# Explicit scheduler priorities, and three ordering rules at the start, in an attention + MLP kernel on one Trainium2 core

## The chip, the cores and the metric

The kernel runs on one core of one Trainium2 chip. Times are device microseconds (us). A verdict compares the fast-state executions of two kernels that ran on the same chip in the same rounds; executions of one kernel here spread over about 1% (355.8 to 360.2 us for the kernel before), so differences under about 1 us are not settled by these runs. Engine names in the profile: PE is TensorE's matmuls, PEld its weight loads, DVE VectorE, ACT ScalarE, POOL GpSimd, SP the engine that issues most DMAs.

## The reference, cut to what matters

```python
# 4 batches, 8 heads, 768 positions, head dimension 64
ub    = sum(max(q*k_min, q*k_max))          # bound of each key chunk of 32, causal
sel   = the 6 chunks with the largest bound, per query
attn  = softmax(mask(scale * q @ k.T, sel and causal)) ; x = attn @ v
x     = x reordered to (4*768 tokens, 512)
h     = x @ w_in                             # 512 -> 2048
g     = where(h > 0, h, exp(min(h, 0)) - 1)  # called ELU below
out   = g @ w_out                            # 2048 -> 512, float32
```

## The kernel before

The work is cut into 8 blocks: 4 batches times 2 halves of 384 query positions. Each block goes through a *front* (K and Q are transposed on TensorE, the chunk bounds `ub` are computed, VectorE selects the chunks), an *attention* (scores `sps`, exponential `pt` on ScalarE, product `o3` with V) and an *MLP* (16 groups `fc` of 4 matmuls into `h_ps`, an ELU over three engines, then 48 matmuls into `o_ps`). The code is traced once; a scheduler orders each engine's instructions at build time, by priority (so far, the order of the code) and by its own model of when data will be ready. How the chip keeps to that order is read from the traces below: in the kernel before, GpSimd stands 22.1 us at one instruction of its order, and a later one that is ready from 35.3 us on starts only at 47.67 us.

```python
    ldpool = pool("ldpool", 4)     # loads of K, Q, V: 4 tiles each
    psM = pool("psM", 4, space=bass.MemoryType.PSUM)     # h_ps and o_ps share 4 banks
    ...
    def cast_v(t, hf):             # V to bfloat16, on GpSimd
        return nc.gpsimd.tensor_scalar(out=vexts[t % NSET][...], in0=ldv.pop((t, hf)), ...)
    ...
    def mlp(b, hf):
        for fc in range(NFC):      # 16
            for kk in range(NKK):  # 4
                nc.tensor.matmul(hw, lhsT=w_in_sb[...], rhs=xT[NPAIR * b + kk, hf], ...)   # L310
            nc.scalar.activation(out=e_sb, in_=hw, func=AF.Exp)                            # L313
            nc.gpsimd.tensor_scalar(out=e_sb, in0=e_sb, scalar1=-1.0, ...)                 # L314
            nc.vector.scalar_tensor_tensor(out=gT[:, fc, :], in0=hw, in1=e_sb, ...)        # L316
        for tt in range(3):
            for fc in range(NFC):
                nc.tensor.matmul(o_ps, lhsT=gT[...], rhs=w_out_sb[:, fc, :], ...)          # L321
            nc.scalar.activation(out=o_sb, in_=o_ps, func=AF.Copy)                         # L324
            nc.sync.dma_start(out=out[r0:r0 + P, :], in_=o_sb)
    ...
    front(0); casts = vpart(0)                       # vpart: the four cast_v of a block
    # load w_in, w_out behind casts[1] and casts[3] on GpSimd's queue
    for i in range(8):
        # attend(block i)
        # load V of block i+1;  front(i+1), which first loads K, Q of block i+2
        # mlp(block i-1)
        # vpart(i+1)
```

The softmax here doesn't subtract the row's maximum and nothing guards it: scores larger than these inputs give would overflow.

Of the kernel before, what the change touches and what calls it, by code (L numbers as in the profile page):

```python
# [25 lines left out]
P = 128  # L26
# [7 lines left out]

NPAIR = H // 2
PE_T = (0, 7)
NSET = 8
Q0 = TOPK * CHUNK
QLO = (Q0, HS)
# [4 lines left out]
def kernel(  # L44
# [31 lines left out]
    nc.scalar.activation(out=warm, in_=warm, func=AF.Exp)  # L76


    def load_one(x, t, hf, name, eng=None):
        b, r = divmod(t, NPAIR)  # L80
        xp = ldpool.tile([P, 3, 2, D], F32, name=name)
        for h in range(2):
            (eng or nc.sync).dma_start(out=xp[:, :, h, :],
                              in_=x[b, 2 * r + h, HS * hf:HS * (hf + 1)].rearrange("(n p) d -> p n d", p=P))
        return xp

    ldk, ldq, ldv = {}, {}, {}

    def load_qk(t, hf):
        ldk[t, hf] = load_one(k, t, hf, "k_pair")  # L90
        ldq[t, hf] = load_one(q, t, hf, "q_pair", nc.scalar if (t < 2 and hf == 0) else nc.sync)

    def load_v(t, hf):
        ldv[t, hf] = load_one(v, t, hf, "v_pair")

    for t in range(NPAIR):
        load_qk(t, 0)
# [52 lines left out]
    wo = moe_w_out.rearrange("(k p) f -> p k f", p=P)  # L150

    def load_w_in(i):
        nc.gpsimd.dma_start(out=w_in_sb[:, :, 512 * i:512 * (i + 1)], in_=wi[:, :, 512 * i:512 * (i + 1)])

    def load_w_out(i):
        nc.gpsimd.dma_start(out=w_out_sb[:, 4 * i:4 * i + 4, :], in_=wo[:, 4 * i:4 * i + 4, :])
# [80 lines left out]
             1: [[(0, 384, 384, 0)], [(1, 384, 384, 0)], [(2, 384, 384, 0)],  # L237
                 [(3, 384, 384, 0), (5, 640, 128, 384)], [(4, 512, 256, 0)]]}

    def attend(t, hf, via_pe):  # L240
        s = t % NSET
        xt = xtpool.tile([P, HS], BF16, name="xt")
        xT[t, hf] = xt
        seg = {}
        for segs in steps[hf]:
            wtot = max(pc + w for (_k, _c, w, pc) in segs)
            pt = ptpool.tile([P, 2, 512], BF16, name="pt")
            both = wtot <= 256
            for hd in range(2):
                if not (both and hd == 1):  # L250
                    sps = psS.tile([P, 512], F32, name="sps")
                o = 256 * hd if both else 0
                for (kb, c0, w, pc) in segs:
                    nc.tensor.matmul(sps[:, o + pc:o + pc + w], lhsT=lhs[s][hd][0:96, P * kb:P * (kb + 1)],  # L254
                                     rhs=rhs[s][hd][0:96, c0:c0 + w], start=True, stop=True)
                if not both:
                    nc.scalar.activation(out=pt[:, hd, 0:wtot], in_=sps[:, 0:wtot],  # L257
                                         func=AF.Exp, scale=SCALE)
            if both:
                nc.scalar.activation(out=pt[:, :, 0:256],  # L260
                                     in_=sps[:, :].rearrange("p (h w) -> p h w", h=2),
                                     func=AF.Exp, scale=SCALE)
            dg = [pc for (kb, c0, w, pc) in segs if c0 == P * kb]
            if len(dg) == 2:
                view = pt[:, :, :].rearrange("p h (x w) -> p h x w", w=P)[:, :, ::3, :]
                nc.vector.tensor_tensor(  # L266
                    out=view, in0=view,
                    in1=tri01[:, :].rearrange("p (a b w) -> p a b w", a=1, b=1)
                    .to_broadcast([P, 2, 2, P]), op=AOT.mult)
            elif dg:  # L270
                view = pt[:, :, dg[0]:dg[0] + P]
                nc.vector.tensor_tensor(  # L272
                    out=view, in0=view,
                    in1=tri01[:, :].rearrange("p (a w) -> p a w", a=1).to_broadcast([P, 2, P]),
                    op=AOT.mult)
            for (kb, c0, w, pc) in segs:
                seg[kb] = (pt, pc - c0)
        o3 = psO.tile([P, 2, 3, D + 1], F32, name="o3")
        for hd in range(2):
            for qi in range(3):  # L280
                qt = 3 * hf + qi
                for kb in range(qt + 1):
                    pt, off = seg[kb]
                    nc.tensor.matmul(o3[:, hd, qi, :],  # L284
                                     lhsT=pt[:, hd, P * qt + off:P * qt + off + P],
                                     rhs=vexts[s][:, kb, hd, :], start=(kb == 0), stop=(kb == qt))
        rcp = opool.tile([P, 2, 3, 1], F32, name="rcp")
        nc.vector.reciprocal(out=rcp, in_=o3[:, :, :, D:D + 1])
        on = opool.tile([P, 3, 2, D], BF16, name="on")
        nc.vector.tensor_tensor(out=on[:, :, :, :].rearrange("p q h d -> p h q d"),  # L290
                                in0=o3[:, :, :, 0:D],
                                in1=rcp[:, :, :, :].to_broadcast([P, 2, 3, D]), op=AOT.mult)
        if via_pe:
            pool0 = (psM, "psm") if (t < NPAIR and hf == 0) else (psT, "ps")
            pxt = pool0[0].tile([P, HS], BF16, name="pxt", tag=pool0[1])
            for qi in range(3):
                nc.tensor.transpose(pxt[:, P * qi:P * (qi + 1)], on[:, qi, :, :], ident_b)
            nc.vector.tensor_copy(out=xt, in_=pxt)
            return
        nc.sync.dma_start_transpose(out=xt[:, :].rearrange("p (n t) -> p n t", n=3),  # L300
                                    in_=on[:, :, :, :].rearrange("p q h d -> p (q h d)"))


    def mlp(b, hf):
        gT = gtpool.tile([P, NFC, HS], BF16, name="gT")
        for fc in range(NFC):
            h_ps = psM.tile([P, 512], F32, name="h_ps", tag="psm")
            hw = h_ps[:, 0:HS]
            for kk in range(NKK):
                nc.tensor.matmul(hw, lhsT=w_in_sb[:, kk, P * fc:P * (fc + 1)],  # L310
                                 rhs=xT[NPAIR * b + kk, hf], start=(kk == 0), stop=(kk == NKK - 1))
            e_sb = mlppool.tile([P, HS], F32, name="e_sb")
            nc.scalar.activation(out=e_sb, in_=hw, func=AF.Exp)  # L313
            nc.gpsimd.tensor_scalar(out=e_sb, in0=e_sb, scalar1=-1.0, scalar2=1.0,  # L314
                                    op0=AOT.add, op1=AOT.mult)
            nc.vector.scalar_tensor_tensor(out=gT[:, fc, :], in0=hw, scalar=0.0, in1=e_sb,  # L316
                                           op0=AOT.max, op1=AOT.min)
        for tt in range(3):
            o_ps = psM.tile([P, DMODEL], F32, name="o_ps", tag="psm")
            for fc in range(NFC):  # L320
                nc.tensor.matmul(o_ps, lhsT=gT[:, fc, P * tt:P * (tt + 1)], rhs=w_out_sb[:, fc, :],  # L321
                                 start=(fc == 0), stop=(fc == NFC - 1))
            o_sb = mlppool.tile([P, DMODEL], F32, name="o_sb", bufs=2)
            nc.scalar.activation(out=o_sb, in_=o_ps, func=AF.Copy)  # L324
            r0 = b * S + hf * HS + P * tt
            nc.sync.dma_start(out=out[r0:r0 + P, :], in_=o_sb)


    blocks = [(b, hf) for b in range(B) for hf in range(2)]

    def pairs_of(b):
        return range(NPAIR * b, NPAIR * (b + 1))

    def front(i):
        b, hf = blocks[i]
        if i + 1 < len(blocks):
            b1, hf1 = blocks[i + 1]
            for t in pairs_of(b1):
                load_qk(t, hf1)
        for t in pairs_of(b):  # L340
            prep(t, hf)
            if i == 0 and t % 2 == 0:
                if t == 0:
                    nc.vector.tensor_copy(out=econst[64:96], in_=eone[64:96].to_broadcast([32, NCH, CHUNK]))
                init_set(t)
                init_set(t + 1)
            if t % 2 == 1:
                select(t // 2, hf)

    def vpart(i):  # L350
        b, hf = blocks[i]
        return [cast_v(t, hf) for t in pairs_of(b)]

    for t in pairs_of(0):
        load_v(t, 0)
    front(0)
    casts = vpart(0)
    with tc.issue_after(casts[1].ins):
        load_w_in(0)
        load_w_in(1)  # L360
    with tc.issue_after(casts[3].ins):
        load_w_in(2)
        load_w_in(3)
        for i in range(4):
            load_w_out(i)
    for i in range(len(blocks)):
        for t in pairs_of(blocks[i][0]):
            attend(t, blocks[i][1], i in PE_T)
        if i == 0:
            for s in range(4, NSET):  # L370
                init_set(s)
        if i + 1 < len(blocks):
            b1, hf1 = blocks[i + 1]
            for t in pairs_of(b1):
                load_v(t, hf1)
            front(i + 1)
        if i >= 1:
            mlp(*blocks[i - 1])
        if i + 1 < len(blocks):
            vpart(i + 1)  # L380
    mlp(*blocks[-1])


# [28 lines left out]
```

## Time and profile before

355.88 us (median of 3, 355.84 to 360.23).

| | PE | DVE | ACT | POOL | mean clock of TensorE |
|---|---|---|---|---|---|
| busy, us of 354.8 | 305.1 (86%) | 220.8 (62%) | 228.6 (64%) | 98.0 (28%) | 0.947 |

Where the time lies in the span is read first. These are lines of the page's second part for the kernel before: the span in 40 slices of 8.9 us, each digit the busy share of a slice in tenths, and below the granted clock and the DMA share (9 is 90% or more).

```profile
PE   4577149799987899998998799998998899999995
POOL 8850065212103310244103310213104311331440
PEclk9855858899999999999999999999999999999999
DMA  7999976644654333251424223222321001000102
```

The fifth digit of PE is 1: a hole from about 36 to 44 us, with GpSimd at 0 in the same slice and the one before it, the DMA share at 9 (1.22 by the windows view of 38 to 42 us), and the clock at half in three slices between 18 and 53 us (the digits 5). The timeline of TensorE in the kernel before shows the hole itself (start, length, line, what it is, count, and in brackets the idle time before it with what ended it).

```profile
36.27 0.55 PE L192 MATMUL psQ<-ident_f,q_pair 128*128 128x128 f32 x3
36.65 0.33 PE L310 MATMUL h_ps<-xt,w_in_sb 128*128 128x384 bf16 x1
48.83 1.44 PE L310 MATMUL h_ps<-xt,w_in_sb 128*128 128x384 bf16 x4 [11.85 <-DVE gT L316]
```

TensorE stops after 16 matmuls of the first MLP, which is 4 groups, as many as `psM` has banks. It waits for `gT`, which frees a bank. `gT` needs GpSimd's `e_sb`, so GpSimd's timeline is next.

```profile
22.47 0.15 POOL L125 MEMSET vext_171<- 128x12 bf16 x1
44.73 0.51 POOL L159 TENSOR_SCALAR vext_129<-v_pair 128x384 bf16<-128x384 f32 x1 [22.11 <-DMA v_pair<-in_v_dram]
...
47.67 0.51 POOL L314 TENSOR_SCALAR e_sb<-e_sb 128x384 f32<-128x384 f32 x1
```

GpSimd stands at the cast of block 1's V from 22.6 to 44.7 us because that V has not landed. The MLP's `e_sb`, whose input ScalarE had finished at 35.3 us, is behind four such casts in GpSimd's order. GpSimd kept to that order in this trace: the `e_sb`, ready at 35.3 us, started at 47.67 us.

Later in the span the losses are smaller. The windows view of the kernel before, over two whole blocks (from the end of one MLP to the end of the next but one), gives busy time and count of each engine, clock, DMA share and GB/s.

```profile
218.90:297.10 78.20, 72.48 (x577) 39.18 (x575) 52.24 (x166) 55.90 (x127) 16.28 (x32) 1.00 0.20 51
```

And one line of TensorE's timeline in it: 42 `o_ps` matmuls in one run, while ScalarE has nothing but `o_sb` to do.

```profile
252.20 9.24 PE L321 MATMUL o_ps<-w_out_sb,gT 128*128 128x512 bf16 x42
```

### The profile page before, as it was taken

What the parts mean: (1) busy time and instruction counts of PE and PEld (TensorE: products, weight loads), DVE (VectorE), ACT (ScalarE), POOL (GpSimd) and SP (SyncE); (2) the same over time, 40 slices, a digit from 0 to 9 for tenths busy, and PEclk for the clock granted to TensorE, in tenths of its full rate; (3) what the DMA queues carried; (4) which work ended last, traced back from release to release, by engine and by line L of the source; (5) the groups of instructions that cost most, each with busy time, mean ns of one, the idle gap of its engine ahead of it and who ended that gap; (6) DMA issues with size and microseconds to landing.
All of it is one profiled execution on the core that took longest, in us unless ns stands there. A gap on an engine that the chain in (4) does not pass through costs nothing.

```text
span 354.8 us, 6831 instructions
## 1 busy us (share of the span) xinstructions
PE 305.1 (86%) x2328; PEld 165.1 (47%) x2328; DVE 220.8 (62%) x690; ACT 228.6 (64%) x506; POOL 98.0 (28%) x219
## 2 busy tenths in 40 slices
PE   4577149799987899998998799998998899999995
PEld 2344024355554444555455345555454445554552
DVE  6877027875659786568748874559747963562450
ACT  5652306889588755998559754998458736982541
POOL 8850065212103310244103310213104311331440
PEclk9855858899999999999999999999999999999999
DMA  7999976644654333251424223222321001000102
GB/s 177 178 202 196 211 167 137 144 100 102 173 141 91 68 71 119 59 133 35 102 84 86 58 68 108 56 47 59 87 72 22 2 30 61 1 3 31 59 5 84
DMA packets 94498, 32.16 MB, mean 91 GB/s; under 512 B 87296, under 2 KB 91392, under 8 KB 94464
## 3 DMA queue, kind: packets, MB, share of 16 engines
q1 hardware_dynamic: 88640, 27.15, 31.9%
q0 software_dynamic: 4224, 4.19, 7.1%
q10 hardware_dynamic: 1600, 0.39, 0.5%
q8 instruction: 18, 0.29, 0.3%
q14 instruction: 16, 0.13, 0.1%
HBM read 27.26 MB, written 6.29 MB: 95 GB/s over the span
## 4 chain that ended last, share of the span: by engine, by line
PE 33%; ACT 16%; DVE 8%; issue 2%; POOL 1%; ACTq 0%; POOLq 0%
PE o_ps L321 18%; PE h_ps L310 7%; ACT pt L257 6%; ACT e_sb L313 3%; PE sps L254 3%; DVE gT L316 2%; PE ub L214 2%; ACT pt L260 2%; PE psK L173 1%; POOL e_sb L314 1%; PE psQ L192 1%; ACT QTf L193 1%; DVE kmm L175 1%; ACT o_sb L324 1%; DVE on L290 1%
## 5 line engine op out<-in xcount | busy, mean ns | idle before, releaser
L310 PE MATMUL h_ps<-xt,w_in_sb 128*128 128x384 bf16 x512 | 113.5, 336 | 17.2 <-DVE gT L316 17.0
L314 POOL TENSOR_SCALAR e_sb<-e_sb 128x384 f32<-128x384 f32 x128 | 65.1, 516 | 190.9 <-ACT e_sb L313 158.3
L316 DVE SCALAR_TENSOR_TENSOR gT<-h_ps,e_sb 128x384 bf16<-128x384 f32 x128 | 69.1, 550 | 52.2 <-POOL e_sb L314 50.4
L321 PE MATMUL o_ps<-w_out_sb,gT 128*128 128x512 bf16 x384 | 90.1, 379 | 0.0
L257 ACT ACTIVATE pt<-sps 128x384 bf16<-128x384 f32 (+1 forms) x160 | 80.1, 547 | 11.4 <-PE sps L254 10.5
L313 ACT ACTIVATE e_sb<-h_ps 128x384 f32<-128x384 f32 x128 | 61.0, 498 | 36.7 <-PE h_ps L310 36.0
L310 PEld LDWEIGHTS <-w_in_sb 128*128 128x128 bf16 x512 | 49.1, 100 | 50.5 <-issue 29.0
L321 PEld LDWEIGHTS <-gT 128*128 128x128 bf16 x384 | 36.8, 98 | 42.3 <-issue 3.5
L324 ACT ACTIVATE o_sb<-o_ps 128x512 f32<-128x512 f32 x24 | 14.3, 597 | 53.8 <-PE o_ps L321 50.0
L284 PEld LDWEIGHTS <-pt 128*128 128x128 bf16 x672 | 29.2, 100 | 17.2 <-DVE pt L266 5.7
L173 PE MATMUL psK<-ident_f,k_pair 128*128 128x128 f32 x96 | 19.2, 306 | 8.7 <-DMA k_pair<-in_k_dram 6.1
L175 DVE TENSOR_REDUCE kmm<-psK 128x12 f32<-128x384 f32 x32 | 17.6, 551 | 6.9 <-PE psK L173 6.3
L266 DVE TENSOR_TENSOR pt<-pt,tri_196 128x512 bf16<-128x512 bf16 x32 | 13.5, 421 | 12.8 <-ACT pt L257 12.6
L192 PE MATMUL psQ<-ident_f,q_pair 128*128 128x128 f32 x96 | 18.2, 295 | 3.7 <-ACT lhs_167 L178 0.8
L260 ACT ACTIVATE pt<-sps 128x512 bf16<-128x512 f32 x32 | 19.4, 606 | 1.2 <-PE sps L254 0.9
L173 PEld LDWEIGHTS psK<-ident_f,k_pair 128*128 128x128 f32 x96 | 11.6, 152 | 16.4 <-issue 5.1
L193 ACT ACTIVATE QTf<-psQ 128x192 f32<-128x192 f32 (+1 forms) x32 | 13.4, 418 | 8.3 <-PE psQ L192 7.9
L192 PEld LDWEIGHTS psQ<-ident_f,q_pair 128*128 128x128 f32 x96 | 10.7, 145 | 16.0 <-ACT lhs_143 L178 2.8
L196 DVE TENSOR_SCALAR Qrl<-QTf 128x192 f32<-128x192 f32 (+1 forms) x32 | 10.3, 323 | 11.7 <-ACT QTf L193 11.1
L176 DVE TENSOR_REDUCE kmm<-psK 128x12 f32<-128x384 f32 x32 | 17.5, 548 | 0.0
L217 DVE STREAM_TRANSPOSE ubT<-ub 128x192 f32<-128x192 f32 (+1 forms) x16 | 7.6, 478 | 10.1 <-PE ub L214 10.1
L272 DVE TENSOR_TENSOR pt<-pt,tri_196 128x256 bf16<-128x256 bf16 x32 | 9.8, 306 | 4.6 <-ACT pt L260 3.8
(348 smaller groups left out, 403.1 us busy)
## 6 DMA issues: line engine op xcount, KB each, us to landing
k_pair<-in_k_dram SPq DMA_DIRECT2D x64, 96.0 KB, 2.5
v_pair<-in_v_dram SPq DMA_DIRECT2D x64, 96.0 KB, 2.4
out_dram<-o_sb SPq DMA_DIRECT2D x24, 256.0 KB, 2.0
q_pair<-in_q_dram SPq DMA_DIRECT2D x60, 96.0 KB, 2.5
w_in_sb<-in_moe_w_in_dram POOLq DMA_DIRECT2D x4, 512.0 KB, 9.9
w_out_sb<-in_moe_w_out_dram POOLq DMA_DIRECT2D x4, 512.0 KB, 20.2
q_pair<-in_q_dram ACTq DMA_DIRECT2D x4, 96.0 KB, 2.9
xt<-on SPq DMA_TRANSPOSE x24, 2.3
```

Of the source, the lines that this page charges most:

```text
L173: nc.tensor.transpose(ps[:, P * n:P * (n + 1)], k_pair[:, n], ident_f)
L175: nc.vector.tensor_reduce(out=kmm[:, 0, :], in_=pv, axis=AX.X, op=AOT.min)
L192: nc.tensor.transpose(ps[:, P * n:P * (n + 1)], q_pair[:, n], ident_f)
L257: nc.scalar.activation(out=pt[:, hd, 0:wtot], in_=sps[:, 0:wtot], func=AF.Exp, scale=SCALE)
L260: nc.scalar.activation(out=pt[:, :, 0:256], in_=sps[:, :].rearrange("p (h w) -> p h w", h=2), func=AF.Exp, scale=SCALE)
L284: nc.tensor.matmul(o3[:, hd, qi, :], lhsT=pt[:, hd, P * qt + off:P * qt + off + P], rhs=vexts[s][:, kb, hd, :], start=(kb == 0), stop=(kb ...
L310: nc.tensor.matmul(hw, lhsT=w_in_sb[:, kk, P * fc:P * (fc + 1)], rhs=xT[NPAIR * b + kk, hf], start=(kk == 0), stop=(kk == NKK - 1))
L313: nc.scalar.activation(out=e_sb, in_=hw, func=AF.Exp)
L314: nc.gpsimd.tensor_scalar(out=e_sb, in0=e_sb, scalar1=-1.0, scalar2=1.0, op0=AOT.add, op1=AOT.mult)
L316: nc.vector.scalar_tensor_tensor(out=gT[:, fc, :], in0=hw, scalar=0.0, in1=e_sb, op0=AOT.max, op1=AOT.min)
L321: nc.tensor.matmul(o_ps, lhsT=gT[:, fc, P * tt:P * (tt + 1)], rhs=w_out_sb[:, fc, :], start=(fc == 0), stop=(fc == NFC - 1))
L324: nc.scalar.activation(out=o_sb, in_=o_ps, func=AF.Copy)
```

## The change

Each block gets a slot of priorities. Attention of block i, front of block i+1 and MLP of block i-1 are spread over the same slot, so that their instructions alternate. These are the *even priorities* of the text below. Three rules concern the start: block 1's loads wait for `w_in` (the *gate*); the V casts of blocks 1 and 2 stand behind the last `e_sb` of the MLP before (the *cast rule*); TensorE's part of front(1) stands behind six groups of MLP(0) (the *front rule*). K and Q are loaded in the slot where they are used, no longer a block ahead. No arithmetic changes. The diff is cut to what matters, so some names in it are set in lines that are left out.

```diff
+GATE = 3
+HGATE = 5
+SP_A = [(0.0, 0.5)] + [(0.0, 0.9)] * 7      # attention's part of its slot
+SP_F = [(0.5, 1.0)] + [(0.0, 0.8)] * 7      # front's
+SP_M = [(0.0, 1.0)] * 8                     # the MLP's, one slot later
 ... (attend, front and mlp call at(f) as they go; loads return their instructions)
+    def span(slot, lo, hi):
+        def at(f):
+            tc.trace_state.cur_priority = int(SLOT * (slot + 1 + lo + (hi - lo) * f))
 ...
     for i in range(len(blocks)):
+        at = span(i, *sp)
         for t in pairs_of(blocks[i][0]):
-            attend(t, blocks[i][1], i in PE_T)
+            attend(t, blocks[i][1], i in PE_T, lambda f, x=x: at(x + f / NPAIR))
+        mm_h, last_e = mlp(*blocks[i], span(i + 1, *SP_M[i]))
         if i + 1 < len(blocks):
-            for t in pairs_of(b1):
-                load_v(t, hf1)
-            front(i + 1)
-        if i >= 1:
-            mlp(*blocks[i - 1])
-        if i + 1 < len(blocks):
-            vpart(i + 1)
-    mlp(*blocks[-1])
+            at = span(i, *SP_F[i])
+            for d in load_block(i + 1):
+                if i == 0:                                   # the gate
+                    tc.add_manual_dep(d.ins, w_ins[GATE].ins.name, SYNC, reason="order")
+            if i == 0:                                       # the front rule
+                with tc.issue_after(mm_h[HGATE].ins):
+                    front(i + 1, at)
+            else:
+                front(i + 1, at)
+            span(i, 0.99, 1.0)
+            for c in vpart(i + 1):
+                if i < 2:                                    # the cast rule
+                    tc.add_manual_dep(c.ins, last_e.ins.name, NOSYNC, reason="order")
```

More of the change, by code (lines that the diff above doesn't have):

```diff
@@ L76, with load_one @@
     nc.scalar.activation(out=warm, in_=warm, func=AF.Exp)
-    def load_one(x, t, hf, name, eng=None):
+    ldk, ldq, ldv = {}, {}, {}
+    def load_one(dst, x, t, hf, name, eng=nc.sync):
         b, r = divmod(t, NPAIR)
         xp = ldpool.tile([P, 3, 2, D], F32, name=name)
-        for h in range(2):
-            (eng or nc.sync).dma_start(out=xp[:, :, h, :],
+        dst[t, hf] = xp
+        return [eng.dma_start(out=xp[:, :, h, :],
                               in_=x[b, 2 * r + h, HS * hf:HS * (hf + 1)].rearrange("(n p) d -> p n d", p=P))
-        return xp
-    ldk, ldq, ldv = {}, {}, {}
+                for h in range(2)]
     def load_qk(t, hf):
-        ldk[t, hf] = load_one(k, t, hf, "k_pair")
-        ldq[t, hf] = load_one(q, t, hf, "q_pair", nc.scalar if (t < 2 and hf == 0) else nc.sync)
+        first = t < 2 and hf == 0
+        return (load_one(ldk, k, t, hf, "k_pair")
+                + load_one(ldq, q, t, hf, "q_pair", nc.scalar if first else nc.sync))
     def load_v(t, hf):
-        ldv[t, hf] = load_one(v, t, hf, "v_pair")
+        return load_one(ldv, v, t, hf, "v_pair")
     for t in range(NPAIR):
@@ L152, in load_w_in @@
     def load_w_in(i):
-        nc.gpsimd.dma_start(out=w_in_sb[:, :, 512 * i:512 * (i + 1)], in_=wi[:, :, 512 * i:512 * (i + 1)])
+        return nc.gpsimd.dma_start(out=w_in_sb[:, :, 512 * i:512 * (i + 1)], in_=wi[:, :, 512 * i:512 * (i + 1)])
     def load_w_out(i):
@@ L238, with attend @@
                  [(3, 384, 384, 0), (5, 640, 128, 384)], [(4, 512, 256, 0)]]}
-    def attend(t, hf, via_pe):
+    def attend(t, hf, via_pe, at):
         s = t % NSET
@@ L244, in attend @@
         seg = {}
-        for segs in steps[hf]:
+        nst = len(steps[hf]) + 1
+        for si, segs in enumerate(steps[hf]):
+            at(si / nst)
             wtot = max(pc + w for (_k, _c, w, pc) in segs)
@@ L277, in attend @@
                 seg[kb] = (pt, pc - c0)
+        at((nst - 1) / nst)
         o3 = psO.tile([P, 2, 3, D + 1], F32, name="o3")
@@ L301, in attend, with mlp @@
                                     in_=on[:, :, :, :].rearrange("p q h d -> p (q h d)"))
-    def mlp(b, hf):
+    def mlp(b, hf, at):
         gT = gtpool.tile([P, NFC, HS], BF16, name="gT")
+        mm_h = []
         for fc in range(NFC):
+            at(0.5 * fc / NFC)
             h_ps = psM.tile([P, 512], F32, name="h_ps", tag="psm")
@@ L309, in mlp @@
             for kk in range(NKK):
-                nc.tensor.matmul(hw, lhsT=w_in_sb[:, kk, P * fc:P * (fc + 1)],
-                                 rhs=xT[NPAIR * b + kk, hf], start=(kk == 0), stop=(kk == NKK - 1))
+                mm = nc.tensor.matmul(hw, lhsT=w_in_sb[:, kk, P * fc:P * (fc + 1)],
+                                      rhs=xT[NPAIR * b + kk, hf], start=(kk == 0), stop=(kk == NKK - 1))
+            mm_h.append(mm)
             e_sb = mlppool.tile([P, HS], F32, name="e_sb")
             nc.scalar.activation(out=e_sb, in_=hw, func=AF.Exp)
-            nc.gpsimd.tensor_scalar(out=e_sb, in0=e_sb, scalar1=-1.0, scalar2=1.0,
+            last_e = nc.gpsimd.tensor_scalar(out=e_sb, in0=e_sb, scalar1=-1.0, scalar2=1.0,
                                     op0=AOT.add, op1=AOT.mult)
@@ L318, in mlp @@
         for tt in range(3):
+            at(0.5 + tt / 6)
             o_ps = psM.tile([P, DMODEL], F32, name="o_ps", tag="psm")
@@ L326, in mlp @@
             nc.sync.dma_start(out=out[r0:r0 + P, :], in_=o_sb)
+        return mm_h, last_e
     blocks = [(b, hf) for b in range(B) for hf in range(2)]
@@ L332, in pairs_of, with load_block, front @@
         return range(NPAIR * b, NPAIR * (b + 1))
-    def front(i):
+    def load_block(i):
         b, hf = blocks[i]
-        if i + 1 < len(blocks):
-            b1, hf1 = blocks[i + 1]
-            for t in pairs_of(b1):
-                load_qk(t, hf1)
+        ins = []
         for t in pairs_of(b):
+            ins += load_qk(t, hf)
+        for t in pairs_of(b):
+            ins += load_v(t, hf)
+        return ins
+    def front(i, at):
+        b, hf = blocks[i]
+        for t in pairs_of(b):
+            at((t % NPAIR) / NPAIR)
             prep(t, hf)
@@ L352, in vpart @@
         return [cast_v(t, hf) for t in pairs_of(b)]
+    SYNC = mybir.DependencyInfo(mybir.DependencyClass.Sync, mybir.DependencyReason.DATA)
+    NOSYNC = mybir.DependencyInfo(mybir.DependencyClass.NoSync, mybir.DependencyReason.DATA)
+    SLOT = 1000000
+    def span(slot, lo, hi):
+        def at(f):
+            tc.trace_state.cur_priority = int(SLOT * (slot + 1 + lo + (hi - lo) * f))
+        at(0.0)
+        return at
     for t in pairs_of(0):
         load_v(t, 0)
-    front(0)
+    front(0, span(-1, 0.0, 0.9))
     casts = vpart(0)
+    w_ins = []
     with tc.issue_after(casts[1].ins):
-        load_w_in(0)
-        load_w_in(1)
+        w_ins += [load_w_in(0), load_w_in(1)]
     with tc.issue_after(casts[3].ins):
-        load_w_in(2)
-        load_w_in(3)
+        w_ins += [load_w_in(2), load_w_in(3)]
         for i in range(4):
@@ L366 @@
     for i in range(len(blocks)):
+        sp = SP_A[i]
+        at = span(i, *sp)
         for t in pairs_of(blocks[i][0]):
-            attend(t, blocks[i][1], i in PE_T)
+            x = (t % NPAIR) / NPAIR
+            attend(t, blocks[i][1], i in PE_T, lambda f, x=x: at(x + f / NPAIR))
         if i == 0:
@@ L371 @@
                 init_set(s)
+        mm_h, last_e = mlp(*blocks[i], span(i + 1, *SP_M[i]))
         if i + 1 < len(blocks):
-            b1, hf1 = blocks[i + 1]
-            for t in pairs_of(b1):
-                load_v(t, hf1)
-            front(i + 1)
-        if i >= 1:
-            mlp(*blocks[i - 1])
-        if i + 1 < len(blocks):
-            vpart(i + 1)
-    mlp(*blocks[-1])
+            at = span(i, *SP_F[i])
[11 more added lines that the diff above has]
+                    tc.add_manual_dep(c.ins, last_e.ins.name, NOSYNC, reason="order")
 _INS = ['q', 'k', 'v', 'moe_w_in', 'moe_w_out']
```

## The prediction

> **What bounds the kernel now.** TensorE. The page's busy table has PE at 305.1 of 354.8 us (86%), ACT 64%, DVE 62%. Busy is not peak, so I rebuilt the streaming work from the timeline and the chain: h_ps matmuls come every 0.163 us (64 in 10.40 us), o_ps every 0.216 us (48 in 10.36 us), so the MLP is 83 + 83 us; sps about 36, o3 25, float32 transposes (192 at 0.138) 26, ub 19. Estimated floor: 273 us. The other 82 us are three losses.
>
> 1. Start (0 to 32 us), before the first MLP matmul: block 0's serial chain. About 24 us lost.
> 2. Hole (32 to 72 us). In the timeline PE stops at 37.0 us and resumes at 48.8 (11.85 us, "h_ps <- DVE gT"). The chain behind it: gT waits for GpSimd's e_sb; GpSimd, in order, sits 22.1 us (to 44.7) on the cast of block 1's V, whose DMA landed late because SP's issues of block 1's K, Q, V, from 16.8 us, share a full DMA system with the weights (windows: DMA share 1.22, about 196 GB/s from 16 to 42 us). w_in's last piece lands at about 29.7 us. [...] the windows give PEclk 0.50 from 42 to 54 us, and again near 66. [...] Some 18 us of streaming happens in these 40.
> 3. Steady state. A batch (two blocks) takes 78.3 us (208.7 to 287.0) for about 68 us of streaming. ACT is at 95-100% from 219 to 243 us while PE has small gaps; from 252 to 261 PE runs 42 o_ps matmuls in one go while ACT idles. Unbalanced, about 10 us a batch.
> The tail (320 to 351 us) is dense MLP.
>
> **What the change does.** No arithmetic or traffic goes. (a) Block 1's loads wait for w_in; w_in whole near 25 us, I expect. (b) V casts of blocks 1 and 2 stand behind the last e_sb of the MLP before, so GpSimd no longer blocks on V. (c) Front(1)'s PE work follows six fc groups of MLP(0). (d) Priorities spread an MLP, an attention and a preparation evenly over a slot.
>
> **Critical path.** The hole is wholly on it. h_ps should still start near 32 us, then run with no wait over 2 us; block 1's front overlaps it, limited by DVE (about 9 us gT plus 16 us preparation). I expect 12 to 16 us back, of it about 4 clock. In steady state interleaving should return 2 to 3 us of the 10 per batch, 3.5 batches: 7 to 11 us; not all, since single-buffered psT and psO remain. Sum 24 us off: **332 us, range 320 to 345. Faster by over 2%: 0.93; within 2%: 0.05; slower: 0.02.**
>
> **What would show it.** PE's 11.85 us wait and GpSimd's 22 us wait gone; w_in landing earlier; PEclk 1.0 from about 40 us on; PE busy total down to about 298 at a span near 331; batch period 75 to 76 us; no o_ps runs of 30 to 40 with idle ACT outside the tail; first 32 us unchanged.
>
> **What would make it wrong.** The delayed K/Q/V of block 1 becoming the new hole (front(1) starved at 38 us): gain under 8 us. Interleaving breaking dense o_ps runs and making PE wait in order for ACT: steady gain zero or negative, near 343. Or batches near 72: about 320.

12 to 16 us for the hole and 7 to 11 us for the steady state make 19 to 27, of which I took 24, and 356 less 24 is 332. The 4 us of clock inside the first term are an estimate, from the halved clock that the windows of the kernel before show from 42 to 54 us and again near 66 us.

## More of the kernel before

To follow progress I use the last eviction `o_sb` of an MLP as a milestone. These are the ones of MLP(1), (3), (5), (6) and (7) in ScalarE's timeline of the kernel before.

```profile
139.30 0.60 ACT L324 ACTIVATE o_sb<-o_ps 128x512 f32<-128x512 f32 x1 [3.71 <-issue]
...
218.29 0.60 ACT L324 ACTIVATE o_sb<-o_ps 128x512 f32<-128x512 f32 x1 [2.90 <-PE o_ps L321]
...
296.52 0.60 ACT L324 ACTIVATE o_sb<-o_ps 128x512 f32<-128x512 f32 x1 [2.91 <-PE o_ps L321]
330.51 0.60 ACT L324 ACTIVATE o_sb<-o_ps 128x512 f32<-128x512 f32 x1 [2.90 <-PE o_ps L321]
351.27 0.60 ACT L324 ACTIVATE o_sb<-o_ps 128x512 f32<-128x512 f32 x1 [2.86 <-PE o_ps L321]
```

From MLP(3) to MLP(5), two blocks take 78.2 us; the last MLP takes 20.8 us.

## The result, and the profile after

The changed kernel takes 338.03 us (median of 4, 337.05 to 340.03) against 356.45 us (median of 4 in the same rounds). The ratio is 0.9469, with a 95% interval of 0.9388 to 0.9551: faster, by 18.4 us. Ratios in this text are the mean time of one kernel's fast runs over that of the other's of the same rounds, so not quite the ratio of the medians. A repeat gave 0.9478 (0.9440 to 0.9516). PE is busy 303.8 of 338.3 us (90%), ACT 68%, DVE 66%, POOL 29%.

The same lines of the page's second part for the changed kernel (slices of 8.5 us):

```profile
PE   3776999998899979999989998999999998999895
POOL 8750442000055214641153003420053004400530
PEclk9955799999999998999999999999999999999999
DMA  7899977542422677566232313223200111000001
```

The 1 in PE's line is gone; the clock is back at 9 in the sixth slice rather than the ninth, and stays at 8 or 9. TensorE's timeline of the changed kernel at that place has no wait over 0.3 us:

```profile
32.56 6.50 PE L321 MATMUL h_ps<-xt,w_in_sb 128*128 128x384 bf16 x24
38.90 0.49 PE L179 MATMUL psK<-ident_f,k_pair 128*128 128x128 f32 x3
39.23 2.11 PE L321 MATMUL h_ps<-xt,w_in_sb 128*128 128x384 bf16 x12
41.57 0.81 PE L321 MATMUL h_ps<-xt,w_in_sb 128*128 128x384 bf16 x4 [0.23 <-DVE gT L328]
```

GpSimd's timeline shows why: it still idles from 22.3 us on, but what it stands at now is the MLP's `e_sb`, and the casts of block 1 come after the last of them.

```profile
22.15 0.16 POOL L131 MEMSET vext_171<- 128x12 bf16 x1
34.99 0.51 POOL L326 TENSOR_SCALAR e_sb<-e_sb 128x384 f32<-128x384 f32 x1 [12.69 <-ACT e_sb L325]
...
49.55 0.99 POOL L326 TENSOR_SCALAR e_sb<-e_sb 128x384 f32<-128x384 f32 x2 [1.54 <-ACT e_sb L325]
50.50 0.52 POOL L165 TENSOR_SCALAR vext_129<-v_pair 128x384 bf16<-128x384 f32 x1
```

In the steady state, the windows view over the same two blocks, and the longest run of `o_ps` in the changed kernel between 218 and 280 us:

```profile
201.90:277.50 75.60, 71.52 (x579) 39.44 (x578) 53.02 (x167) 57.00 (x127) 16.57 (x32) 1.00 0.20 53
```

```profile
224.81 3.01 PE L334 MATMUL o_ps<-w_out_sb,gT 128*128 128x512 bf16 x13
```

The period is 75.6 us instead of 78.2, and the longest run is 13 instead of 42. The milestones of the changed kernel:

```profile
123.09 0.60 ACT L337 ACTIVATE o_sb<-o_ps 128x512 f32<-128x512 f32 x1 [4.45 <-PE o_ps L334]
...
201.30 0.60 ACT L337 ACTIVATE o_sb<-o_ps 128x512 f32<-128x512 f32 x1 [2.84 <-PE o_ps L334]
...
276.94 0.60 ACT L337 ACTIVATE o_sb<-o_ps 128x512 f32<-128x512 f32 x1 [3.12 <-PE h_ps L321]
311.74 0.60 ACT L337 ACTIVATE o_sb<-o_ps 128x512 f32<-128x512 f32 x1 [0.69 <-PE o_ps L334]
334.78 0.60 ACT L337 ACTIVATE o_sb<-o_ps 128x512 f32<-128x512 f32 x1 [2.86 <-PE o_ps L334]
```

Subtracting line by line, the lead over the kernel before is 16.2 us at MLP(1), 17.0 at MLP(3), 19.6 at MLP(5), 18.8 at MLP(6) and 16.5 at the end. Read so, nearly all of the gain is at the start, little comes in the steady state, and the tail gives some of it back: the last MLP takes 23.0 us instead of 20.8. That reading was my first theory, and the experiments did not leave it whole.

### The profile page after: what moved, and what is told of

It reads as the page before. It is cut to its first block, busy times and chain, and to the rows that moved or that the text cites. A ratio compares the mean times of both kernels' runs of the same rounds, so it can differ in the third digit from the quotient of the medians.

```text
span 338.3 us, 6875 instructions
## 1 busy us (share of the span) xinstructions
PE 303.8 (90%) x2328; PEld 165.8 (49%) x2328; DVE 223.2 (66%) x690; ACT 231.4 (68%) x506; POOL 98.3 (29%) x219
## 4 chain that ended last, share of the span: by engine, by line
PE 32%; DVE 24%; issue 18%; ACT 17%; POOL 5%; DMA 3%; SPq 0%; POOLq 0%; ACTq 0%
PE o_ps L334 11%; PE h_ps L321 9%; DVE gT L328 6%; ACT pt L265 5%; ACT e_sb L325 4%; PE sps L262 4%; PE ub L220 3%; POOL e_sb L326 3%; DMA xt<-on 2%; DVE kmm L181 2%; DVE kmm L182 2%; PE psK L179 1%; DVE on L299 1%; DVE ubT L223 1%; DMA v_pair<-in_v_dram 1%
## 5 line engine op out<-in xcount | busy, mean ns | idle before, releaser
L321 PE MATMUL h_ps<-xt,w_in_sb 128*128 128x384 bf16 x512 | 107.1, 334 | 8.3 <-DMA xt<-on 4.6
L334 PE MATMUL o_ps<-w_out_sb,gT 128*128 128x512 bf16 x384 | 99.5, 379 | 0.9 <-DVE gT L328 0.8
L265 ACT ACTIVATE pt<-sps 128x384 bf16<-128x384 f32 (+1 forms) x160 | 79.0, 538 | 16.6 <-PE sps L262 15.3
L334 PEld LDWEIGHTS <-gT 128*128 128x128 bf16 x384 | 35.4, 97 | 36.5 <-issue 3.8
L274 DVE TENSOR_TENSOR pt<-pt,tri_196 128x512 bf16<-128x512 bf16 x32 | 14.3, 446 | 18.8 <-ACT pt L265 18.8
L179 PE MATMUL psK<-ident_f,k_pair 128*128 128x128 f32 x96 | 20.0, 300 | 6.1 <-POOL kst_146 L138 4.1
L268 ACT ACTIVATE pt<-sps 128x512 bf16<-128x512 f32 x32 | 19.5, 609 | 2.6 <-PE sps L262 2.2
L199 ACT ACTIVATE QTf<-psQ 128x192 f32<-128x192 f32 (+1 forms) x32 | 13.2, 413 | 10.1 <-PE psQ L198 7.0
L202 DVE TENSOR_SCALAR Qrl<-QTf 128x192 f32<-128x192 f32 (+1 forms) x32 | 11.7, 365 | 11.5 <-ACT QTf L199 11.0
L280 DVE TENSOR_TENSOR pt<-pt,tri_196 128x256 bf16<-128x256 bf16 x32 | 10.6, 333 | 7.7 <-ACT pt L268 7.7
```

The source lines that it names most:

```text
L179: nc.tensor.transpose(ps[:, P * n:P * (n + 1)], k_pair[:, n], ident_f)
L265: nc.scalar.activation(out=pt[:, hd, 0:wtot], in_=sps[:, 0:wtot], func=AF.Exp, scale=SCALE)
L268: nc.scalar.activation(out=pt[:, :, 0:256], in_=sps[:, :].rearrange("p (h w) -> p h w", h=2), func=AF.Exp, scale=SCALE)
L321: mm = nc.tensor.matmul(hw, lhsT=w_in_sb[:, kk, P * fc:P * (fc + 1)], rhs=xT[NPAIR * b + kk, hf], start=(kk == 0), stop=(kk == NKK - 1))
L334: nc.tensor.matmul(o_ps, lhsT=gT[:, fc, P * tt:P * (tt + 1)], rhs=w_out_sb[:, fc, :], start=(fc == 0), stop=(fc == NFC - 1))
```

## The experiments

All twelve runs gave correct results; single slow executions of the kernel before were left out. *Theory A* below is that the gain is nearly all the removed hole, and the hole is removed by GpSimd's order; rivals are given with each run. The runs went in three calls of four, with the kernel before timed beside each (357.13, 356.77 and 356.40 us).

### Serial priorities, all three rules kept

Attention first, then the front, then the MLP, in every slot but the first.

```diff
-SP_A = [(0.0, 0.5)] + [(0.0, 0.9)] * 7
-SP_F = [(0.5, 1.0)] + [(0.0, 0.8)] * 7
-SP_M = [(0.0, 1.0)] * 8
+SP_A = [(0.0, 0.5)] + [(0.0, 0.3)] * 7
+SP_F = [(0.5, 1.0)] + [(0.3, 0.6)] * 7
+SP_M = [(0.6, 0.95)] * 8
```

> Changed kernel with its three start dependencies kept, but from slot 1 on the priorities put attention first, then the preparation, then the MLP (0 to 0.3, 0.3 to 0.6, 0.6 to 0.95), as the kernel before orders them. Theory A (nearly all of the gain is the hole at the start; the even interleaving returns only about 2 to 3 us): 339 to 343 us, batch period 77 to 79 us. Rival B (interleaving is worth a third or more of the gain, as the prediction had it): 345 us or more.

Measured: 357.38 us, ratio 1.0001 (0.9968 to 1.0034). The whole gain was gone, a plain miss for theory A. The hole was not back: the longest wait of `h_ps` for `gT` was 2.2 us. The time was lost later: the milestone of MLP(1) came at 126.94 us, 12.4 before the kernel before, but MLP(2) then took 51.0 us against 43.0, and MLP(3) to MLP(5) took 82.0 us against 78.2. The clock explains a part of that at most: this trace's clock records have TensorE at half clock for 6.8 us of MLP(2) and 3.4 us of the later pair, where the kernel before has none. Half of these, 3.4 and 1.7 us, is an estimate of the most that they cost, from the spacing of `h_ps` in one run: 0.32 us in the changed kernel's head, where the clock is 0.50 (11 from 32.56 to 35.8 us), and 0.163 us at full clock (64 in 10.40 us in the kernel before).

This run has a fault as a control. The cast rule also binds block 2: its V casts come after the last `e_sb` of MLP(1). Serial priorities want MLP(1) after attention 2, and attention 2 needs those casts. The fifth run below takes that conflict away.

### Loads of block 1 free (no gate)

```diff
-            for d in load_block(i + 1):
-                if i == 0:
-                    tc.add_manual_dep(d.ins, w_ins[GATE].ins.name, SYNC, reason="order")
+            load_block(i + 1)
```

> Changed kernel without the wait of block 1's loads for w_in; instruction order on all engines is the same. Theory A (GpSimd's order made the hole: with the V casts behind the MLP's last e_sb, late V data hurts nobody): within 2 us of the changed kernel, 336 to 340 us, first h_ps still near 32.5 us because the last xT of block 0 is there then and w_in landed at 29.7 us in the kernel before. Rival B (a full DMA system delays the weights and so the MLP; the gate is what pays): 343 us or more, first h_ps or o_ps waiting for a weight DMA.

Measured: 338.41 us, ratio 0.9487 (0.9449 to 0.9524), within 0.4 us of the changed kernel's 338.03, with the same instruction order on all engines. The first `h_ps` is at 32.51 us (32.56 with the gate), and no wait of TensorE for a weight appears. So the gate is worth nothing measurable. `w_in` lands earlier with it (the slowest of the four issues takes 10.9 us to land instead of 14.1), but MLP(0) waits for block 0's last `xt` until 32.5 us anyway.

### V casts free (no cast rule)

```diff
-            for c in vpart(i + 1):
-                if i < 2:
-                    tc.add_manual_dep(c.ins, last_e.ins.name, NOSYNC, reason="order")
+            vpart(i + 1)
```

> Changed kernel with the V casts of blocks 1 and 2 left to the scheduler, which puts the first cast of block 1 behind five e_sb of MLP(0); loads still gated. Theory A: GpSimd blocks there from about 39 us until V lands near 46, h_ps stalls some 4 to 7 us, clock falls to half for a few us more: 343 to 348 us. Rival B (the gate pays, not the order): 337 to 340 us.

Measured: 346.16 us, ratio 0.9698 (0.9665 to 0.9730), 7.7 to 8.1 us slower than with the rule (338.41 in the run beside it, 338.03 for the changed kernel). GpSimd's timeline of this run, then TensorE's:

```profile
36.67 1.81 POOL L326 TENSOR_SCALAR e_sb<-e_sb 128x384 f32<-128x384 f32 x3 [0.69 <-ACT e_sb L325]
45.70 0.52 POOL L165 TENSOR_SCALAR vext<-v_pair 128x384 bf16<-128x384 f32 x1 [7.22 <-DMA v_pair<-in_v_dram]
```

```profile
38.18 2.11 PE L321 MATMUL h_ps<-xt,w_in_sb 128*128 128x384 bf16 x12
47.34 1.44 PE L321 MATMUL h_ps<-xt,w_in_sb 128*128 128x384 bf16 x4 [7.04 <-DVE gT L328]
```

One cast that waits 7.22 us for its V makes a hole of 7.04 us on TensorE four groups later. The four `h_ps` after it take 1.44 us, as do the four after the hole of the kernel before, where the clock is 0.50; four in the changed kernel's trace above (41.57 us) take 0.81 us. The hole follows GpSimd's order, with the gate in place. Theory A holds here.

### Front(1) free on TensorE (no front rule)

```diff
-            if i == 0:
-                with tc.issue_after(mm_h[HGATE].ins):
-                    front(i + 1, at)
-            else:
-                front(i + 1, at)
+            front(i + 1, at)
```

> Changed kernel without TensorE's order of block 1's preparation behind six fc groups of MLP(0). Some K transposes of block 1 then stand before block 0's attention on TensorE and wait for loads that are gated to about 28 us. Theory A: TensorE stalls up to 10 us in block 0's attention (k_pair wait), first h_ps at 38 to 42 us, total 343 to 350 us. Rival: attention of block 0 is slow anyway and the stall hides: 337 to 341 us.

Measured: 350.03 us, ratio 0.9811 (0.9763 to 0.9859): below 1, but the verdict at 2% is unclear. One line of TensorE's timeline tells it:

```profile
36.48 0.87 PE L179 MATMUL psK<-ident_f,k_pair 128*128 128x128 f32 x3 [9.93 <-DMA k_pair<-in_k_dram]
```

The scheduler put a K transpose of block 1 in the middle of attention 0, and the gate held that K back (its loads are issued from 27.1 us on). The first `h_ps` moved from 32.6 to 42.8 us. The gate makes the front rule necessary.

### Serial priorities, cast rule for block 1 alone

The first experiment again with one more edit:

```diff
-                if i < 2:
+                if i < 1:
```

> Serial priorities as in the first run, but V casts stand behind the MLP's last e_sb for block 1 alone. In the first run the same rule for block 2 makes attention 2 wait for MLP(1), which serial priorities put last: that cost 8 us there and upset the order after it (its batches took 82 us). Here TensorE's order from block 4 on is that of the kernel before. Theory A (the gain of the change is the start; even interleaving adds only 0 to 3 us in all): 338 to 343 us, batch period 78 us as before. Rival B (without interleaving the start's gain is lost later, as the first run suggests): 350 us or more.

Measured: 347.58 us, ratio 0.9761 (0.9726 to 0.9796): 9.8 us better than the first run, from a rule on four casts. In the traces, the last 1,500 or so of TensorE's 2,328 matmuls now stand in the same order as in the kernel before (in the first run only the last 200 or so; single records are missing from these traces). The loads of K and Q, which the changed code issues in another slot, also come as in the kernel before in this stretch: those between 192 and 240 us are the ones between 202 and 250 us there, each 10.0 us earlier to within 0.3 us. So this is the start's repair alone, followed by the old steady state. The time fell between the two theories, a miss for both: the start is worth about half of the gain.

### Even priorities alone

No gate, no cast rule, no front rule.

> Changed kernel with the even priorities alone: loads free, casts free, front free. Theory A: the hole at the start is back (GpSimd waiting for V under the MLP's e_sb) and only the steady state's 2.6 us a batch, less about 2 at the tail, remains: 350 to 356 us. Rival B (interleaving is what pays): 343 us or less.

Measured: 350.30 us, ratio 0.9841 (0.9799 to 0.9882): below 1, but the verdict at 2% is unclear. The hole is back, as this line of the waits shows (total, times, longest):

```profile
PE h_ps L321 <- DVE gT L328: 16.4, 9, 11.8
```

The interleaving therefore brings about 6 us without any repair of the start. With the run before it, this fills a table of two by two; in brackets the gain as one minus the ratio, times 356.5 us.

| | order of the kernel before or serial | even priorities |
|---|---|---|
| start not repaired | 356.4 to 357.1 | 350.30 (5.7) |
| start repaired | 347.58 (8.5) | 338.49 (18.6) |

8.5 and 5.7 make 14.2, but both together give 18.6. Each part is worth some 4 us more when the other is there (4.4, with about 2.4 either way if the three half-intervals are added in quadrature; the cells were timed each against the kernel before). The lower right cell has the cast rule for block 2 as well; the last run below shows that this makes no difference. The milestones say where (lead over the kernel before at the last `o_sb` of each MLP, from one profile each; "changed, repeat" is the changed kernel):

| lead, us | MLP(1) | MLP(3) | MLP(5) | MLP(6) | MLP(7) |
|---|---|---|---|---|---|
| start repaired alone | 10.5 | 10.0 | 8.5 | 8.5 | 8.5 |
| even priorities alone | 2.9 | 6.9 | 9.8 | 8.7 | 6.4 |
| both (changed) | 16.2 | 17.0 | 19.6 | 18.8 | 16.5 |
| both (changed, repeat) | 17.0 | 19.5 | 22.0 | 21.2 | 19.0 |

The start's repair gives its lead once and never adds to it; its fall from 10.0 to 8.5 us comes in a stretch that has 3.4 us of half clock in this trace (271.8 to 275.2 us) and none in the kernel before. The even priorities add 2.5 to 4.0 us to the lead in each of the two pairs of blocks from MLP(1) to MLP(5) (only 0.8 in the first pair of one profile, where the clock was at half from 126.25 to 129.66 us), and lose 3.1 to 3.4 us between MLP(5) and the end. The extra of both together is there by MLP(1): 16.2 and 17.0 us are 2.8 and 3.6 more than 10.5 plus 2.9. What makes it is not shown by a run. The clock may have a share: the fifth run's trace is at half clock from 84.0 to 87.4 us, where the traces of the changed kernel are at full clock, but half of that, 1.7 us, is the most that this stretch explains. The end of an MLP is also not the whole state of the work, since the order of the kernel before runs attention further ahead of the MLPs. This stays open.

### Last-but-one MLP spread further, to fill the tail

```diff
-SP_M = [(0.0, 1.0)] * 8
+SP_M = [(0.0, 1.0)] * 6 + [(0.15, 1.3)] + [(0.0, 1.0)]
```

> Changed kernel with MLP(6) spread over 0.15 to 1.3 of its slot, so that 20 of its o_ps are left to fill TensorE while block 7's last xT is made. In the changed kernel the last MLP takes 23.0 us against 20.8 before, the difference being a wait for xT. Expected: 1.5 to 2.5 us less than the changed kernel, 335 to 337 us. Rival (the work just moves, attention 7 gets no shorter): no change.

Measured: 336.74 us, ratio 0.9459 (0.9424 to 0.9495), beside 338.21 for the next run, which equals the changed kernel. About 1.5 us, at the lower edge of what was expected, and within the spread of the runs. The profile puts it where it was meant to be: from MLP(5) to the end it takes 56.4 us, against 57.8 for the changed kernel and 54.8 for the kernel before, and TensorE is idle in that stretch for 1.6, 3.0 and 0.4 us.

### Mask copies moved from VectorE to GpSimd

```diff
-            nc.vector.tensor_copy(out=lhs[s][h][64:96, :],
+            (nc.gpsimd if s >= 4 else nc.vector).tensor_copy(out=lhs[s][h][64:96, :],
```

> Changed kernel with the eight mask copies of sets 4 to 7 moved from VectorE (0.35 us each, between 20 and 32 us, among block 0's attention) to GpSimd, which is idle from 22 to 34 us. If VectorE paces block 0's attention, first h_ps comes 1 to 2.5 us earlier and the total falls by as much: 335.5 to 337 us. If TensorE at half clock and latencies pace it: within 0.5 us of the changed kernel.

Measured: 338.21 us, ratio 0.9489 (0.9460 to 0.9518), no gain. In the profile the first `e_sb` starts at 34.15 us, 34.41 in the changed kernel. So these copies do not hold block 0's attention back. The profile of this run also holds a trap, its clock line:

```profile
PEclk9999999999999999999999999999999999999999
```

It reads as full clock in the head (before the first `h_ps`), where the changed kernel's trace has half clock from 17.0 to 37.5 us. But the clock records of this trace begin only at 35.5 us, with a change to full clock, and the page counts the time before them as full. The matmuls themselves say half clock (the tile view of `h_ps` on TensorE, count and ns min/median/max; the first line from the window 32.3 to 35 us, the second from 36 to 38 us):

```profile
L321 PE MATMUL h_ps<-xt,w_in_sb x9: 527/527/527, 32.3 to 34.9; 128*128 128x384 bf16 x9
L321 PE MATMUL h_ps<-xt,w_in_sb x12: 326/326/326, 35.8 to 37.6; 128*128 128x384 bf16 x12
```

The same matmul takes 527 ns in the changed kernel's head too. So the mean clock of 1.000 that this execution is given (337.23 us; the others, at 0.969 to 0.983, took 337.67 to 338.61) says nothing of the head, and no run here shows what half clock there costs.

### The changed kernel again

> The changed kernel itself, on the chip of the three runs beside it: 337 to 339 us.

Measured: 338.49 us, ratio 0.9478 (0.9440 to 0.9516).

### The cast rule as the only rule at the start

Even priorities, no gate, no front rule.

> Changed kernel with even priorities and the V cast rule, but loads free and block 1's preparation free on TensorE. Theory: the cast rule alone removes the hole; TensorE's order was needed only because the gate makes K late (that run stalled 9.9 us on k_pair), so without the gate the first K transposes of block 1 wait about 2 us as in the kernel before: 338 to 342 us. Rival (the order of block 1's preparation behind six fc groups is worth something of itself): 344 us or more.

Measured: 339.73 us, ratio 0.9517 (0.9473 to 0.9561), 1.2 us behind the changed kernel beside it, intervals overlapping. Without the gate the early K transpose costs little:

```profile
14.74 0.52 PE L179 MATMUL psK<-ident_f,k_pair 128*128 128x128 f32 x3 [1.02 <-DMA k_pair<-in_k_dram]
```

No wait of `h_ps` for `gT` exceeds 1.0 us. Beside even priorities alone (350.30, ratio 0.9841), one ordering rule on GpSimd brings about 11 us (10.6 by the medians, 11.6 by the ratios); gate and front rule together bring about 1.2, if anything.

### Loads free and the tail filled

> Loads free and the last-but-one MLP spread over 0.15 to 1.3. The gate is worth nothing and the tail 1.1 to 1.5 us: 336 to 337.5 us, 1 to 2 us under the changed kernel beside it.

Measured: 337.19 us (336.52 to 337.69), ratio 0.9446 (0.9411 to 0.9481), against 338.49 (337.11 to 339.39) for the changed kernel beside it. This is the best candidate, simpler by one rule and some 1.3 us lower, but the ranges overlap and 0.4% is not settled.

### Cast rule for block 1 alone, even priorities

> Changed kernel with the cast rule for block 1 alone. With even priorities MLP(1)'s e_sb are early in the slot, so the rule for block 2 should cost little, unlike with serial priorities: within 1.5 us of the changed kernel beside it. Rival (it holds attention 2 back as it did there): 3 us or more faster.

Measured: 337.52 us (337.35 to 341.02), ratio 0.9480 (0.9435 to 0.9525), the same as the changed kernel. The rule for block 2, which cost 9.8 us under serial priorities, costs nothing measurable when the MLP is spread over its slot.

## Why the prediction was right or wrong

The time came within the range (338.0 in 320 to 345) and the direction was right; the gain was 18.4 us where 24 was expected.

- *What bounds the kernel* was right: TensorE, with a hole, and the hole's chain (gT, GpSimd, V's DMA) was the true one. The run without the cast rule shows each link.
- *"(a) Block 1's loads wait for w_in"* was put down as part of the repair. It brings nothing, as the run with free loads shows. The prediction named the full DMA system as part of the chain, and the trace fits that: block 1's K and Q took up to 17 us to land, against at most 3.3 for block 0's, and SP came to block 1's V only from 36.2 us on. No run takes the load off to show it. But with the cast rule GpSimd does not wait for that V (the four casts run from 50.50 us on without a gap), so making the loads orderly has no more effect.
- *"12 to 16 us back, of it about 4 clock"*: the start repaired brings 8.5 us alone, and 12.9 on top of even priorities (0.9841 less 0.9478, of 356.5). The size is right only in the company of the other part. The clock's share is not shown: the mean clock rose from 0.947 to 0.964 only. An estimate from the clock records: the kernel before worked at half clock from 48.8 to 55.3 us and from 65.5 to 68.9 us, which costs at most half of that, 4.9 us (by the spacing of `h_ps` above); the changed kernel has neither stretch. What makes the clock fall is not shown either: in the kernel before it fell at 41.6 us, 4.6 us after TensorE's last matmul, and again at 65.5 us, with TensorE busy for 2.9 of the 5 us before; in the changed kernel it fell at 17.0 us, with TensorE busy for 3.4 of the 5 us before.
- *"2 to 3 us of the 10 per batch, 3.5 batches"* is the step that failed in size. A batch did gain 2.6 us, to 75.6 where 75 to 76 was predicted, but only two whole batches can (MLP(1) to MLP(5): 3.4 us in one profile of the changed kernel and 5.0 in the other). The prediction left the tail out as dense. It is where 3.1 us were lost again: from MLP(5) to the end 57.8 us against 54.8. Even spreading uses up MLP(6)'s `o_ps`, which in the kernel before filled TensorE while block 7 finished. The tail run, which leaves some of them, got about half of that back. In the table of two by two the even priorities are worth 5.7 us alone and 10.1 on top of the repaired start; that the second figure lies in the predicted 7 to 11 is luck, since about 4 us of it is the joint part, which the prediction did not have.
- *"PE busy total down to about 298"* was wrong: 303.8, and 301.4 in the repeat. Idle time fell instead, from 49.7 to 34.5 us. These two lines of the groups, kernel before and changed kernel, show why busy time misleads (busy us, mean ns of one):

```profile
L321 PE MATMUL o_ps<-w_out_sb,gT 128*128 128x512 bf16 x384 | 90.1, 379 | 0.0
```

```profile
L334 PE MATMUL o_ps<-w_out_sb,gT 128*128 128x512 bf16 x384 | 99.5, 379 | 0.9 <-DVE gT L328 0.8
```

  The same 384 matmuls count 9.4 us more when they stand in short runs (103 runs instead of 44): the profile counts 0.379 us for one that stands alone, and in a run they start 0.216 us apart, so 59 more runs of 0.163 us make 9.6.
- *First 32 us unchanged* and *no long o_ps runs* were right (32.56 against 32.37 us for the first `h_ps`; at most 16 in a run before the last MLP, where the kernel before has 33, 34, 42, 34 and 48).

My theory after the result, that the start is nearly everything, fell too: the milestones of one pair of kernels credited to the start what comes from both parts together. Only runs of each part alone showed it.

## What to carry to other kernels

In the kernel before, GpSimd stood 22.1 us at a cast whose V was late, and an `e_sb` behind it that was ready at 35.3 us started at 47.67 us. Look in the order of the idle engine for the first instruction that cannot run, and move that one behind the work that can. Here one such rule on GpSimd was worth about 11 us, and two further rules about loads and TensorE's order about 1.2 together, if anything. Take every ordering rule together with the priorities: the same rule on four casts cost 9.8 us under serial priorities and nothing measurable under even ones. And test each part alone as well as both: here 8.5 and 5.7 us alone made 18.6 together. And before a clock line is believed, look at the time of one matmul: in one profile here a stretch without clock records read as full clock (9) while an `h_ps` matmul took 527 ns, against 326 ns later.
